# Strided heads before local heads, narrower first groups of expert 0, and q scaled by 0.125 on GpSimd when it is loaded

## The chip, the core and the metric

One core of a Trainium2 chip runs the whole program. The metric is the device time of one execution in microseconds (us). The engines are TensorE (PE, its weight loads PEld), VectorE (DVE), ScalarE (ACT), GpSimd (POOL) and SyncE (SP, which issues most transfers). Each engine works through its own list of instructions in the listed order.

## The reference

Attention over 2 images, 8 heads, 576 tokens of 64 dimensions: heads 0 to 3 see the last 32 tokens (local), heads 4 to 7 the earlier tokens of the same class modulo 32 (strided). Then a dense mixture of 8 experts whose weights P come from 8 rounds of row and column normalisation, and a second mixture that takes the two best experts of each token.

```python
scores = scale * np.matmul(q, k.transpose(0, 1, 3, 2))          # scale = 1/8
scores = np.where(masks[None, :, :, :], scores, -1000000000.0)
attn = np.exp(scores - np.max(scores, axis=-1, keepdims=True))
attn = attn / (np.sum(attn, axis=-1, keepdims=True) + 1e-09)
x = np.matmul(attn, v)                                           # heads side by side: 1152 x 512
P = np.exp(x @ w_gate - max)                                     # 8 rounds over rows, then columns
out = sum over e of P[:, e:e + 1] * (np.maximum(x @ w1[e], 0.0) @ w2[e])
```

The second mixture (`_moe2_ref`) is not touched.

## The kernel before

Products are made from a high and a low part of each operand (`split`: ACT writes the high part, DVE the low part), so that one wide product is three matmuls (`mm3`).

**Attention, one image at a time.** `attention(b)` runs two head pairs of local heads (`local_unit`, three groups of three blocks of 64 queries, six units in an image), then the strided heads (`strided_unit`, three units, each of both head pairs). Each unit does: mask and score matmuls into a PSUM bank (`scores`), row maxima on DVE (L241), the maxima times 0.125 on DVE (L242), exponentials with sums on ACT (L247, scale 0.125), then on DVE 1e-9 added to the sums (L248), reciprocals (L249) and the product (L251); transposes on PE into `tr`, a copy to `at` on ACT and DVE in turn, value matmuls into `ot`, and a split into `xh` and `xl`. The score banks come from the tags in `where[1]`: "ad" gives four banks, "a" two. It is set to "a" after image 0.

**Expert 0 is computed in an early and a late half.** While the attention of image 1 still runs, `pair1` and `pair2` make the hidden rows `gh`, `gl` (products `h`) and the outputs `y` for the tokens in `early`, then, after the gate and its rounds (`sinkhorn`, one matmul `cs` in each of the 8 rounds), those in `late`. Conversions of a weight block `raw` to `u1h`, `u1l`, `u2h`, `u2l` are placed behind the attention's splits (`firsts[8]` and later). `sums()` prepares `r`, `sh` and `sl` for experts 1 to 6, whose products are `a`, `b`, `c`, `d` (L715).

The order on each engine is fixed when the program is built: a scheduler goes by its own times of instructions, and `tc.issue_after` holds some back. The lines that the steps speak of:

```python
early = ((0, 512),)
late = ((512, 320), (832, 320))
    with tc.issue_after(marks[1]), tc.issue_after(lows[0].ins):
        sums()
```

Of the kernel before, what the change touches and what calls it, by code (L numbers as in the profile page):

```python
# [9 lines left out]
F32 = mybir.dt.float32  # L10
# [4 lines left out]
AF = mybir.ActivationFunctionType  # L15
# [5 lines left out]
STRIDE = 32  # L21
# [24 lines left out]
MASKED = -8.0e9  # L46
# [16 lines left out]
def tile_kernel(ctx: ExitStack, tc: tile.TileContext, qL, kL, vL, qS, kS, vS, wg, u12, w1, w2, wgn, noise, v1, v2, cst, masks, dummy, out):  # L63
# [117 lines left out]
    where = [0, "ad", None]  # L181
# [4 lines left out]
    def load_pair(b, hp):  # L186
        local = hp < 2
        nq, nk, nb, q, k, v = (NQ, LK, NJ, qL, kL, vL) if local else (GK, GK, NG, qS, kS, vS)
        hp %= 2
        flip[1] = (flip[1] + 1) % 4  # L190
        qs = acc[:, 4:].rearrange("p t d -> p (t d)")[:, flip[1] * 640:flip[1] * 640 + nb * nq]
        w = k.shape[-1]
        if b == 0 and not local:
            qs = pre.tile([128, NG * GK], F32, name=f"qs{hp}")
            ks = pre.tile([128, S + STRIDE], F32, name=f"ks{hp}")
        else:
            ks = apool.tile([128, S + STRIDE], F32, tag="ks", name="ks")
        if local or hp == 0:
            where[2] = (pre if b == 0 and not local else apool).tile([128, NG, 128], F32, tag="vs", name="vs")
        vs, n = where[2], v.shape[-2]  # L200
        if b == 0 and hp == 0 and local:
            cut = 3 * nq
            nc.sync.dma_start(ks[:, :224], k[b, hp, :, :224])
            nc.sync.dma_start(qs[:, :cut], q[b, hp, :, :cut])
            nc.sync.dma_start(ks[:, 224:w], k[b, hp, :, 224:])
            nc.sync.dma_start(qs[:, cut:], q[b, hp, :, cut:])
        else:
            nc.sync.dma_start(ks[:, :w], k[b, hp])
            nc.sync.dma_start(qs, q[b, hp])

        def values():
            if local:
                nc.sync.dma_start(vs[:, :n], v[b, hp])
            elif hp == 1:
                nc.sync.dma_start(vs[:, :n], v[b])

        return (qs, ks, vs), values
# [44 lines left out]
    def local_unit(b, hp, j0, nb, got):  # L262
        qs, ks, vs = got
# [18 lines left out]
    def strided_unit(b, j0, nb, pairs):  # L282
        mask = maskb[:, None, M_MS:].to_broadcast([128, nb, GK])
        scv = [scores(GK, GK, mask, j0, nb, qs, ks, GK) for qs, ks, _ in pairs]
        vs = pairs[0][2]
# [19 lines left out]
    def load_first():  # L305
        pairs, queue = [], []
        for hp in range(4):
            got, values = load_pair(0, hp)
            pairs.append(got)
            if queue:  # L310
                queue.pop(0)()
            queue.append(values)
        queue.pop()()
        return pairs

    def attention(b):
        pairs = load_first() if b == 0 else []

        def get(hp):
            while hp >= len(pairs):  # L320
                got, values = load_pair(b, len(pairs))
                values()
                pairs.append(got)
            return pairs[hp]
# [28 lines left out]
    where[1] = "a"  # L353
# [264 lines left out]
    early = ((0, 512),)  # L618
    late = ((512, 320), (832, 320))
# [27 lines left out]
    for q in range(NP):  # L647
        raw = fetch_u(0, q)
        with tc.issue_after(firsts[min(q, 1) * 3 + 8].ins):
            a, b = conv_u1(raw[0]), conv_u2(raw[1])  # L650
        pair1(a, early)
        for t in range(4):
            pair2(b, t, None, q == 0)
# [13 lines left out]
    def sums():  # L667
        with tc.tile_pool(name="tpool", bufs=1, side="right", reuse_waits="tile") as tpool:
            for c in range(2):
                r = tpool.tile([128, 4, HALF], F32, tag="r", name="r")  # L670
                for i in range(4):
                    nc.vector.tensor_tensor(r[:, i], quarter[0][i][:, c].bitcast(F32), quarter[1][i][:, c].bitcast(F32), op=ALU.add)
                for o, x, y, op in ((3, 2, 3, ALU.add), (2, 0, 2, ALU.subtract), (0, 3, 0, ALU.subtract), (1, 1, 0, ALU.subtract)):
                    nc.vector.tensor_tensor(r[:, o], r[:, x], r[:, y], op=op)
                for k, i in enumerate((3, 0, 2, 1)):
                    split(sh[:, k, c], sl[:, k, c], r[:, i])

    marks = []
    for q in range(NP):
        q = NP - 1 - q  # L680
        if q < NP - 1:
            raw = fetch_u(0, q)
            a, b = conv_u1(raw[0]), conv_u2(raw[1])
        pair1(a, late)
        for t in range(4, NT):
# [448 lines left out]
_HOST = ["qL", "kL", "vL", "qS", "kS", "vS", "wg", "u12", "w1", "w2", "wgn", "noise", "v1", "v2", "cst", "masks", "dummy"]  # L1134


def layout(x):
# [10 lines left out]
    def keys(a):  # L1148
        return a.transpose(0, 1, 3, 2).reshape(B, 2, 2 * D, a.shape[2])
# [25 lines left out]
    for j in range(3):  # L1175
# [15 lines left out]
    d = dict(qL=keys(q[:, :4]), kL=keys(kL), vL=values(vL, LK, NQ),  # L1191
             qS=keys(qS), kS=keys(kS), vS=values(vS, GK, GK).reshape(B, 128, NG, 2 * D), wg=rows(x["moe_w_gate"]),
# [22 lines left out]
```

## Time and profile before

| | before |
|---|---|
| median of 3 runs | 1104.33 us (1103.67 to 1104.6) |
| profiled execution, its time | 1105.53 us |
| span of the profiled execution | 1103.7 us |
| PE busy, share of the span | 1085.4 us, 98% |
| PEld | 954.5 us, 86% |
| DVE | 661.6 us, 60% |
| ACT | 396.5 us, 36% |
| POOL | 158.8 us, 14% |
| TensorE's granted clock, mean | 0.992 of full speed |

PE has work nearly all the time. A matmul's shown duration overlaps the next one, so that a busy PE is not a PE at its best: the spacing of starts tells more. Whatever is lost is lost in the first 180 us. The granted clock is there in fractions of 2.4 GHz, and 0.50 is 1.2 GHz.

### The profile page before, as it was taken

Reading aid. Unit: us, or ns where it says so; the run is one execution under the profiler, and the core shown is the slowest. Engines: PE = TensorE matmul, PEld = TensorE weight load, DVE = VectorE, ACT = ScalarE, POOL = GpSimd, SP = SyncE. Lnnn points to the kernel's source line nnn. Section 1 sums busy time; section 2 is a strip of 40 time slices with the busy share of each in tenths; the row PEclk is TensorE's granted clock in tenths of the full one; section 3 lists DMA queues with packets and bytes.
Section 4 is the critical chain, followed back from the end, with each engine's and each line's share of the span. In section 5 each row is a group of like instructions: output and inputs, shape, how many; then the busy total and the mean of one; then the engine's idle time right before and its main releaser. Section 6 shows DMA issues by size and latency. Waiting matters only on the chain.

```text
span 1103.7 us, 17178 instructions
## 1 busy us (share of the span) xinstructions
PE 1085.4 (98%) x6840; PEld 954.5 (86%) x6840; DVE 661.6 (60%) x1359; ACT 396.5 (36%) x893; POOL 158.8 (14%) x182
## 2 busy tenths in 40 slices
PE   9999999999999999999999999999999999999996
PEld 6778988999899999899999999988888888888885
DVE  6865896666666666666666666554266465445440
ACT  6641334332322333322332332222133254444541
POOL 1000112111111111121111120000041432232211
PEclk9999999999999999999999999999999999999998
DMA  9321162111111121111121111122103674666531
GB/s 349 133 77 39 39 198 67 39 71 44 40 39 39 39 78 39 39 39 39 39 77 39 39 39 39 39 77 77 39 21 125 181 256 106 205 204 205 185 99 24
DMA packets 31589, 98.18 MB, mean 89 GB/s; under 512 B 6482, under 2 KB 15186, under 8 KB 22928
## 3 DMA queue, kind: packets, MB, share of 16 engines
q1 hardware_dynamic: 16192, 78.94, 19.7%
q0 software_dynamic: 5408, 11.26, 4.9%
q10 hardware_dynamic: 9904, 6.83, 2.0%
q8 instruction: 55, 0.90, 0.3%
q14 instruction: 30, 0.25, 0.1%
HBM read 85.51 MB, written 11.60 MB: 88 GB/s over the span
## 4 chain that ended last, share of the span: by engine, by line
PE 90%; DVE 3%; DMA 2%; ACT 2%; issue 1%; POOL 1%; POOLq 0%; SPq 0%; ACTq 0%
PE y L164 42%; PE h L164 17%; PE a L715 14%; PE b L715 7%; PE d L715 3%; PE y L892 2%; PE xgt L800 1%; PE sc L232 1%; ACT spread L247 1%; DMA raw<-in_v 1%; DMA xg<-x2d,tt 1%; DVE wl L106 1%; PE sc L221 0%; POOL table L548 0%; PE lgT L367 0%
## 5 line engine op out<-in xcount | busy, mean ns | idle before, releaser
L641 DVE SCALAR_TENSOR_TENSOR acc<-y,P,acc 128x512 f32<-128x512 f32 x207 | 152.8, 748 | 142.8 <-PE y L164 142.7
L164 PE MATMUL y<-u2h,gh 128*128 128x512 f32 x504 | 199.0, 395 | 0.6 <-DVE acc L641 0.3
L164 PE MATMUL y<-u2l,gh 128*128 128x512 f32 x504 | 197.8, 392 | 0.0
L164 PE MATMUL y<-u2h,gl 128*128 128x512 f32 x504 | 190.6, 393 | 0.8 <-DVE gl L102 0.8
L154 POOL TENSOR_TENSOR ut<-raw 128x256 f32<-128x256 f32 x48 | 36.5, 782 | 554.0 <-DVE u1l L106 446.0
L164 PEld LDWEIGHTS y<-u2h,gl 128*128 128x128 f32 x504 | 94.8, 189 | 20.8 <-DVE gl L102 1.6
L164 PE MATMUL h<-xh,wh 128*128 128x384 f32 (+8 forms) x352 | 110.2, 313 | 0.2 <-DVE hl L102 0.2
L164 PE MATMUL h<-xl,wh 128*128 128x384 f32 (+8 forms) x352 | 110.2, 313 | 0.0
L164 PE MATMUL h<-xh,wl 128*128 128x384 f32 (+8 forms) x352 | 109.8, 312 | 0.0
L164 PEld LDWEIGHTS y<-u2h,gh 128*128 128x128 f32 x504 | 95.1, 189 | 16.2 <-issue 0.7
L164 PEld LDWEIGHTS y<-u2l,gh 128*128 128x128 f32 x504 | 95.0, 188 | 14.1
L101 ACT ACTIVATE hh<-h 128x256 fp32r<-128x256 f32 (+2 forms) x88 | 35.6, 415 | 95.5 <-PE h L164 95.5
L164 PEld LDWEIGHTS h<-xh,wh 128*128 128x128 f32 x352 | 66.4, 189 | 1.1 <-DVE hl L102 0.5
L164 PEld LDWEIGHTS h<-xl,wh 128*128 128x128 f32 x352 | 66.4, 189 | 0.9 <-issue 0.4
L104 ACT ACTIVATE u2h<-raw 128x1024 fp32r<-128x1024 f32 x31 | 33.0, 1064 | 94.5 <-PE y L164 90.8
L164 PEld LDWEIGHTS h<-xh,wl 128*128 128x128 f32 x352 | 66.4, 189 | 0.0
L102 DVE SCALAR_TENSOR_TENSOR hl<-h,hh 128x256 fp32r<-128x256 f32 (+2 forms) x88 | 40.3, 465 | 41.2 <-ACT hh L101 41.2
L106 DVE TENSOR_TENSOR wl<-raw,wh 128x1024 fp32r<-128x1024 f32 x42 | 49.5, 1221 | 22.8 <-ACT wh L104 22.8
L715 PE MATMUL b<-sh,u1h 128*128 128x288 f32 x192 | 57.5, 299 | 0.0
L715 PE MATMUL b<-sl,u1h 128*128 128x288 f32 x192 | 57.5, 299 | 0.0
L715 PE MATMUL b<-sh,u1l 128*128 128x288 f32 x192 | 57.4, 299 | 0.0
L715 PE MATMUL a<-sh,u1l 128*128 128x288 f32 x192 | 57.0, 297 | 0.0
(257 smaller groups left out, 2453.9 us busy)
## 6 DMA issues: line engine op xcount, KB each, us to landing
raw<-in_u SPq DMA_DIRECT2D x31, 1024.0 KB, 4.8
raw<-in_v SPq DMA_DIRECT2D x20, 1024.0 KB, 8.9
acc<-in_v SPq DMA_DIRECT2D x12, 1024.0 KB, 6.8
raw<-in_w SPq DMA_DIRECT2D x4, 1024.0 KB, 4.9
out<-zero ACTq DMA_DIRECT2D x1, 3072.0 KB, 18.2
vs<-in_vL SPq DMA_DIRECT2D x4, 576.0 KB, 7.1
x2d<-acc ACTq DMA_DIRECT2D x9, 256.0 KB, 2.0
vs<-in_vS SPq DMA_DIRECT2D x2, 704.0 KB, 6.5
```

What stands on the lines that cost most here:

```text
L101: seen[0] = nc.scalar.activation(hi, src, AF.Relu)
L102: lows.append(nc.vector.scalar_tensor_tensor(lo, src, 0.0, hi.bitcast(F32), op0=ALU.max, op1=ALU.subtract))
L104: seen[0] = nc.scalar.activation(hi, src, AF.Copy)
L106: nc.vector.tensor_tensor(lo, src, hi.bitcast(F32), op=ALU.subtract)
L154: nc.gpsimd.tensor_tensor(t[:, o], x, y, op=ALU.subtract)
L164: nc.tensor.matmul(o, a, b, start=start, stop=stop)
L232: nc.tensor.matmul(sc[h * 64:h * 64 + w, i * nk:(i + 1) * nk], qs[r, j * w:(j + 1) * w], ks[r, j * step:j * step + nk], start=False, stop= ...
L247: nc.scalar.activation(s[:, x, i], v[:, i], AF.Exp, scale=0.125, bias=nmx[:, k:k + 1], accum_out=sm[:, k:k + 1])
L641: nc.vector.scalar_tensor_tensor(acc[:, t], p, P[:, t, scale:scale + 1], acc[:, t], op0=ALU.mult, op1=ALU.add)
L715: nc.tensor.matmul(p, l[:, b, c], m, start=first and i == 0, stop=i == 5, skip_group_check=not first)
L800: nc.tensor.transpose(p[:, o:o + 128], xg[:, c * 128:(c + 1) * 128], ident)
L892: nc.tensor.matmul(p[j * w:j * w + k, :d], hr[:, f, :k], raws[f // 4][:, f % 4, j * d:(j + 1) * d], start=f == 0, stop=f == 7)
```

## The change

The strided heads of an image now come first, the local units after them, and of these both head pairs of one group of blocks in turn. Keys and queries come in one tensor per kind (`xS`, `xL`), strided ones of image 0 in two pieces; the queries are multiplied by 0.125 on GpSimd where they land (`scale`, nine instructions more on its list). L242 is gone, and the exponentials have no scale (the mask's constant is an eighth of what it was). The score banks go down to two ("a") already after the first local group of image 0. The early half of expert 0 is 384 tokens and three `y` tiles instead of 512 and four; the late half is two groups of 384 instead of two of 320, with six `y` tiles instead of five. The conversions of the first block are placed behind `firsts[4]` and `firsts[6]`, which are now the last strided unit and the first local one. `sums()` is tied to `marks[0]` and `marks[1]`, one half each.

```diff
-MASKED = -8.0e9
+MASKED = -1.0e9
...
-    def load_pair(b, hp):
...
+    def scale(x):
+        nc.gpsimd.tensor_scalar(x, x, 0.125, None, op0=ALU.mult)
+
+    def load_strided(b):
+        xs = [(pre if b == 0 else apool).tile([128, 2, NG * GK], F32, tag=f"x{hp}" if b == 0 else "x", name="x",
+                                              bufs=2 - (b == 0)) for hp in range(2)]
+        cut = STRIDED[0][1] * GK
+        for p in (slice(0, cut), slice(cut, NG * GK)) if b == 0 else (slice(0, NG * GK),):
+            for hp in range(2):
+                nc.sync.dma_start(xs[hp][:, :, p], xS[b, hp, :, :, p])
+                scale(xs[hp][:, 0, p])
...
+    def load_local(b):
+        xs, vs = [], []
+        for hp in range(2):
+            x = acc[:, 4:].rearrange("p t d -> p (t d)")[:, hp * 1280:hp * 1280 + 2 * S + STRIDE]
+            nc.sync.dma_start(x, xL[b, hp])
+            scale(x[:, :S])
...
-        nc.vector.tensor_scalar(nmx[:, :n], nmx[:, :n], 0.125, None, op0=ALU.mult)
...
-                nc.scalar.activation(s[:, x, i], v[:, i], AF.Exp, scale=0.125, bias=nmx[:, k:k + 1], accum_out=sm[:, k:k + 1])
+                nc.scalar.activation(s[:, x, i], v[:, i], AF.Exp, bias=nmx[:, k:k + 1], accum_out=sm[:, k:k + 1])
...
-        for hp in range(2):
-            for j0, nb in LOCAL:
-                local_unit(b, hp, j0, nb, get(hp))
-        get(3)
+        xs, vs, values = load_strided(b)
+        values()
+        lx, lv = load_local(b)
         for j0, nb in STRIDED:
-            strided_unit(b, j0, nb, pairs[2:])
+            strided_unit(b, j0, nb, xs, vs)
+        for j0, nb in LOCAL:
+            if j0:
+                where[1] = "a"
+            for hp in range(2):
+                local_unit(b, hp, j0, nb, *lx[hp], lv[hp])
...
-    where[1] = "a"
...
-    early = ((0, 512),)
-    late = ((512, 320), (832, 320))
+    early = whole[:1]
+    late = whole[1:]
...
-        with tc.issue_after(firsts[min(q, 1) * 3 + 8].ins):
-            a, b = conv_u1(raw[0]), conv_u2(raw[1])
+        with tc.issue_after(firsts[10 if q else 4].ins):
+            a = conv_u1(raw[0])
+        with tc.issue_after(firsts[10 if q else 6].ins):
+            b = conv_u2(raw[1])
...
+                with tc.issue_after(marks[c]):
+                    r = tpool.tile([128, 4, HALF], F32, tag="r", name="r")
...
-    with tc.issue_after(marks[1]), tc.issue_after(lows[0].ins):
-        sums()
+    sums()
```

On VectorE, among the local units of image 0, the list of before reads as follows (`nmx` are the maxima, `sm` the sums, `s` the weights of a unit; each unit has its own numbers):

```order
L248 TENSOR_SCALAR sm_186<-sm_186 128x3
L241 TENSOR_REDUCE nmx_255<-sc_244 128x3
L249 RECIPROCAL sm_186<-sm_186 128x3
L242 TENSOR_SCALAR nmx_255<-nmx_255 128x3
L251 TENSOR_TENSOR s_182<-s_182,sm_186 128x288
L248 TENSOR_SCALAR sm_222<-sm_222 128x3
L241 TENSOR_REDUCE nmx_289<-sc_280 128x3
```

The maxima of a unit two places on (255) stand between the sum and the product of unit 182. On the same engine, among the local units of image 0, the list now reads:

```order
L106 TENSOR_TENSOR xl_77<-ot_249,xh_76 128x12x18
L244 TENSOR_TENSOR s_397<-s_397,sm_400 128x288
L235 TENSOR_REDUCE nmx_431<-sc_422 128x3
L241 TENSOR_SCALAR sm_433<-sm_433 128x3
L242 RECIPROCAL sm_433<-sm_433 128x3
L106 TENSOR_TENSOR xl_77<-ot_305,xh_76 128x8x18
L244 TENSOR_TENSOR s_430<-s_430,sm_433 128x288
L106 TENSOR_TENSOR u1l_941<-raw_938,u1h_940 128x512 x2
L106 TENSOR_TENSOR xl_77<-ot_306,xh_76 128x8x18
L253 COPY at_411<-tr_407 96x384
L235 TENSOR_REDUCE nmx_464<-sc_455 128x3
```

The maxima of the next unit (431, 464) have moved behind the product of the unit before them, and a weight conversion stands between. On TensorE, at the first wide product of expert 0, before:

```order
L298 MATMUL ot_515<-at_512,vs_119 64x54 x6
L227 LDWEIGHTS mask_sb_103
L227 MATMUL sc_658<-mask_sb_103 128x288
L232 MATMUL sc_658<-ks_653,acc_75 64x96 x6
L227 LDWEIGHTS mask_sb_103
L227 MATMUL sc_692<-mask_sb_103 128x288
L232 MATMUL sc_692<-ks_653,acc_75 64x96 x6
L271 MATMUL tr_604<-cs_78,s_593 96x128 x3
L164 MATMUL h_972<-xh_76,u1h_962 128x512
```

and on TensorE at the same place now:

```order
L221 LDWEIGHTS mask_sb_103
L221 MATMUL sc_561<-mask_sb_103 128x216
L226 MATMUL sc_561<-x_535 54x54 x8
L269 MATMUL ot_479<-at_477,vs_122 64x64 x6
L263 MATMUL tr_506<-cs_78,s_496 96x128 x3
L164 MATMUL h_950<-xh_76,u1h_940 128x384
L164 MATMUL h_950<-xl_77,u1h_940 128x384
```

Before, all of image 0, five score groups of image 1 and two of its transposes stand ahead of the first `h`. Now two score groups of image 1 do, and one value group of image 0 (`ot_512`) comes after it.

## Rows read from the trace of the kernel before

**Rows 1.** Windows of 10 us: stretch, engines' busy us (instructions), clock, DMA share, GB/s.

```profile
10.00:20.00 10.00, 9.96 (x175) 7.26 (x173) 8.24 (x35) 8.65 (x49) 0.00 (x0) 1.00 1.03 411
...
140.00:150.00 10.00, 9.41 (x49) 7.73 (x49) 10.00 (x20) 5.06 (x9) 1.40 (x2) 1.00 0.34 115
...
160.00:170.00 10.00, 9.11 (x50) 7.14 (x49) 9.75 (x28) 3.21 (x7) 3.90 (x4) 1.00 1.03 319
170.00:180.00 10.00, 8.99 (x51) 8.73 (x52) 5.50 (x17) 2.66 (x7) 0.00 (x0) 0.83 0.12 49
```

**Rows 2.** Waits of TensorE in 0 to 200 us: total, times, longest.

```profile
PE cs L395 <- DVE c L393: 1.5, 1, 1.5
...
PE sc L227 <- ACT spread L247: 1.1, 2, 0.6
```

**Rows 3.** Windows of 0.5 us around slow clocks; the clock is third from the end.

```profile
34.50:35.00 0.50, 0.50 (x3) 0.40 (x2) 0.50 (x2) 0.50 (x2) 0.00 (x0) 0.63 0.00 0
...
65.50:66.00 0.50, 0.50 (x3) 0.37 (x3) 0.50 (x3) 0.00 (x0) 0.00 (x0) 0.59 0.00 0
...
68.50:69.00 0.50, 0.50 (x3) 0.40 (x2) 0.00 (x0) 0.50 (x4) 0.00 (x0) 0.50 0.00 0
...
174.50:175.00 0.50, 0.50 (x5) 0.50 (x4) 0.17 (x1) 0.30 (x1) 0.00 (x0) 0.68 0.00 0
```

**Rows 4.** Timeline of ScalarE: start, duration, line, operation, tiles, shapes, count.

```profile
8.18 0.34 ACT L247 ACTIVATE s<-sc,nmx 128x96 f32<-128x96 f32 x1 [6.16 <-DVE nmx L242]
8.51 0.33 ACT L247 ACTIVATE s<-sc,nmx 128x96 f32<-128x96 f32 x1
...
24.22 0.39 ACT L247 ACTIVATE spread<-sc,nmx 128x54 f32<-128x54 f32 x1
...
24.50 0.39 ACT L247 ACTIVATE spread<-sc,nmx 128x54 f32<-128x54 f32 x1
...
31.32 1.18 ACT L104 ACTIVATE u1h<-raw 128x512 fp32r<-128x512 f32 x2
32.35 1.08 ACT L104 ACTIVATE u2h<-raw 128x1024 fp32r<-128x1024 f32 x1
```

**Rows 5.** Timeline of VectorE in the attention of image 0.

```profile
25.97 0.17 DVE L248 TENSOR_SCALAR sm<-sm 128x3 f32<-128x3 f32 x1
26.17 0.18 DVE L249 RECIPROCAL sm<-sm 128x3 f32<-128x3 f32 x1
26.39 0.55 DVE L106 TENSOR_TENSOR xl<-ot,xh 128x216 fp32r<-128x216 f32 x1
26.86 0.43 DVE L251 TENSOR_TENSOR s<-s,sm 128x288 f32<-128x288 f32 x1
...
27.22 0.44 DVE L241 TENSOR_REDUCE nmx<-sc 128x3 f32<-128x288 f32 x1
...
28.59 0.55 DVE L260 COPY at<-tr 96x384 f32<-96x384 f32 x1
...
34.42 1.22 DVE L106 TENSOR_TENSOR u2l<-raw,u2h 128x1024 fp32r<-128x1024 f32 x1
```

**Rows 6.** Timeline of TensorE: a score group up to a transpose, and the first `h`.

```profile
10.27 0.28 PE L227 MATMUL sc<-mask_sb 128*128 128x288 bf16 x1
...
11.13 0.53 PE L271 MATMUL tr<-cs,s 128*96 128x128 f32 x3
...
33.83 0.78 PE L164 MATMUL h<-xh,u1h 128*128 128x512 f32 x1
```

**Rows 7.** GpSimd: a group of instructions (busy, mean ns, idle before), and a timeline row.

```profile
L347 POOL CAST upper<-cs 128x128 bf16<-128x128 f32 x1 | 0.3, 289 | 25.7 <-DMA cs<-in_cst 25.7
...
129.80 2.06 POOL L154 TENSOR_TENSOR ut<-raw,ut 128x256 f32<-128x256 f32 x2
```

**Rows 8.** Timeline of VectorE, one operation beside GpSimd's work and three without.

```profile
131.36 1.11 DVE L106 TENSOR_TENSOR sl<-r,sh 128x576 fp32r<-128x576 f32 x1
...
132.47 2.08 DVE L106 TENSOR_TENSOR sl<-r,sh 128x576 fp32r<-128x576 f32 x3
```

More of the change, by code (lines that the diff above doesn't have):

```diff
@@ L62, in tile_kernel @@
 @with_exitstack
-def tile_kernel(ctx: ExitStack, tc: tile.TileContext, qL, kL, vL, qS, kS, vS, wg, u12, w1, w2, wgn, noise, v1, v2, cst, masks, dummy, out):
+def tile_kernel(ctx: ExitStack, tc: tile.TileContext, xL, vL, xS, vS, wg, u12, w1, w2, wgn, noise, v1, v2, cst, masks, dummy, out):
     nc = tc.nc
@@ L180, in tile_kernel @@
     flip = [0, 0]
-    where = [0, "ad", None]
+    where = [0, "ad"]
     spread = [apool.tile([128, 4, 2, 64], F32, name=f"spread{i}", bufs=1) for i in range(2)]
@@ L184, in tile_kernel @@
         nc.gpsimd.memset(x, 0.0)
-    def load_pair(b, hp):
[L187 to L217, printed above, removed]
@@ new lines, in load_local @@
+    def load_local(b):
[4 more added lines that the diff above has]
+            scale(x[:, :S])
+            xs.append((x[:, :S], x[:, S:]))
+        for hp in range(2):
+            v = apool.tile([128, NG, 128], F32, tag="vs", name="vs", bufs=3)
+            nc.sync.dma_start(v[:, :NJ], vL[b, hp])
+            vs.append(v)
+        return xs, vs
@@ L260, in take, with local_unit @@
             nc.vector.tensor_copy(o, i)
[L262 to L263 removed]
+    def local_unit(b, hp, j0, nb, qs, ks, vs):
         first = maskb[:, M_ML:M_MS].rearrange("p (b k) -> p b k", b=3)
@@ L280, in local_unit, with strided_unit @@
         split(xh[:, hp, o], xl[:, hp, o], ot[:, :nb * NQ])
-    def strided_unit(b, j0, nb, pairs):
+    def strided_unit(b, j0, nb, xs, vs):
         mask = maskb[:, None, M_MS:].to_broadcast([128, nb, GK])
-        scv = [scores(GK, GK, mask, j0, nb, qs, ks, GK) for qs, ks, _ in pairs]
-        vs = pairs[0][2]
+        scv = [scores(GK, GK, mask, j0, nb, x[:, 0], x[:, 1], GK) for x in xs]
         wide = spread[where[0] // 2 % 2]
@@ L303, in strided_unit @@
             split(view[0][:, r0:r1], view[1][:, r0:r1], ot[:, :(r1 - r0) * NI].rearrange("p (r i) -> p r i", i=NI))
[L305 to L314, printed above, removed]
-    def attention(b):
[L317 to L324, printed above, removed]
-        for hp in range(2):
-            for j0, nb in LOCAL:
-                local_unit(b, hp, j0, nb, get(hp))
-        get(3)
-        for j0, nb in STRIDED:
-            strided_unit(b, j0, nb, pairs[2:])
+    def attention(b):
+        xs, vs, values = load_strided(b)
+        values()
+        lx, lv = load_local(b)
+        for j0, nb in STRIDED:
+            strided_unit(b, j0, nb, xs, vs)
+        for j0, nb in LOCAL:
+            if j0:
+                where[1] = "a"
+            for hp in range(2):
+                local_unit(b, hp, j0, nb, *lx[hp], lv[hp])
     mask_sb = apool.tile([128, NMASK // 2], F32, name="mask_sb", bufs=1)
@@ L648, in tile_kernel @@
         raw = fetch_u(0, q)
-        with tc.issue_after(firsts[min(q, 1) * 3 + 8].ins):
-            a, b = conv_u1(raw[0]), conv_u2(raw[1])
+        with tc.issue_after(firsts[10 if q else 4].ins):
+            a = conv_u1(raw[0])
+        with tc.issue_after(firsts[10 if q else 6].ins):
+            b = conv_u2(raw[1])
         pair1(a, early)
-        for t in range(4):
+        for t in range(3):
             pair2(b, t, None, q == 0)
@@ L669, in sums @@
             for c in range(2):
[L670 to L676, printed above, removed]
+                with tc.issue_after(marks[c]):
+                    r = tpool.tile([128, 4, HALF], F32, tag="r", name="r")
+                    for i in range(4):
+                        nc.vector.tensor_tensor(r[:, i], quarter[0][i][:, c].bitcast(F32), quarter[1][i][:, c].bitcast(F32), op=ALU.add)
+                    for o, x, y, op in ((3, 2, 3, ALU.add), (2, 0, 2, ALU.subtract), (0, 3, 0, ALU.subtract), (1, 1, 0, ALU.subtract)):
+                        nc.vector.tensor_tensor(r[:, o], r[:, x], r[:, y], op=op)
+                    for k, i in enumerate((3, 0, 2, 1)):
+                        split(sh[:, k, c], sl[:, k, c], r[:, i])
     marks = []
@@ L684, in tile_kernel @@
         pair1(a, late)
-        for t in range(4, NT):
+        for t in range(3, NT):
             pair2(b, t, None, q == NP - 1)
         marks.append(seen[0].ins)
-    with tc.issue_after(marks[1]), tc.issue_after(lows[0].ins):
-        sums()
+    sums()
     with tc.issue_after(seen[0].ins):
@@ L1190, in layout @@
     dummy[:, 0] = np.arange(E * ROWS) % ROWS % PAD
-    d = dict(qL=keys(q[:, :4]), kL=keys(kL), vL=values(vL, LK, NQ),
-             qS=keys(qS), kS=keys(kS), vS=values(vS, GK, GK).reshape(B, 128, NG, 2 * D), wg=rows(x["moe_w_gate"]),
+    d = dict(xL=np.concatenate([keys(q[:, :4]), keys(kL)], 3), vL=values(vL, LK, NQ),
+             xS=np.stack([keys(qS), keys(kS)], 3), vS=values(vS, GK, GK).reshape(B, 128, NG, 2 * D), wg=rows(x["moe_w_gate"]),
              u12=np.stack([x["moe_w1"].reshape(E, NC, 128, NP, 256).transpose(0, 3, 2, 1, 4).reshape(E, NP, 128, 2, 512),
```

4 lines of the change are left out of this document (3 added, 1 removed).

## The prediction

> **What bounds the kernel now.** The page comes first: TensorE is busy 98% of the span, so a gain has to come from time in which TensorE idles or runs at half its clock. The windows of 10 us show where that is [rows 1]. At 10 to 20 us TensorE counts as busy, but ScalarE is at 8.65 and VectorE at 8.24 of 10 us: there the chain score, maxima, exponentials, product, transpose sets the pace, and TensorE's 175 instructions are small ones. At 140 to 180 us TensorE idles .59, .89 and 1.01 us in three windows while VectorE is full (10.00 and 9.75). The 0.5-us windows add the clock [rows 3]: before 34.5, before 68.5 and before 174.5 us TensorE stood still or did little, and 0.50 to 0.68 of full speed was granted for about 3.3 to 3.7 us each time, which costs half of that, some 1.7 us. After 180 us I found no loss, and from about 215 us on the order of all engines is the same in both kernels. So the change is worth what it does to these first stretches. I went through them by a ledger: the time up to a point less the time that the columns done by then take at full clock. In the kernel before it stands at 9.2 us at 33.8, 12.9 at 70, 15.0 at 150 and 20.1 at 179.
>
> **The change part by part.** The columns of TensorE in sum hardly change: three groups of `h` are 3 x 384 columns instead of 512 + 2 x 320, and `y` has nine tiles in both. What changes is when there is work.
>
> **A, the front: +5.8 us.** I walked the new order by hand with durations of before. Removed: one operation on VectorE of .17 us, by the neighbouring 128x3 operation [rows 5], ahead of each unit's exponentials; the first exponential then starts at about 7.75 instead of 8.18 [rows 4]. The strided exponentials of 54 columns follow each other every .28 us, the local ones of 96 every .32 to .33 [rows 4]. The strided units of image 0 have 22: 7.75 + 22 x .28 = 13.9, and with one copy of .46 on ScalarE the first local unit starts at 14.4. So far nothing is lost. But now every local unit hangs on the one before it. In the kernel before, the maxima of a unit two places on stand between the sum and the product of a unit, so that ScalarE has its next exponentials ready. In the new order the maxima come behind the product of the preceding unit, and often behind its `xl`. One turn is then three exponentials, .95; the sum's tail, .1; the add .20; the reciprocal .22; `xl` .47; the product .36; the reduction .37 [rows 5]; and .1 to start: 2.75 us, in which ScalarE works about a third. From 14.4 two units in stock and then such turns give 18.7, 20.2 and 23.1. The next turn also has two pieces of `u1l` on VectorE, which I take at .6 each (half of the 1.22 us of `u2l`, which has twice the columns [rows 5]), a second `xl` and a copy: 27.9. The last has `u2l` of 1.2 behind `u2h` of 1.08 [rows 4, 5]: 32.1. With its exponentials, sum, `xl`, copy and product it ends at 34.75, its transposes take .46 to .53 [rows 6], and the first `h`, which stands behind these transposes, starts at 35.3 instead of 33.83: 1.5 us later. Less is done by then, too. Before, five score groups of image 1 of .86 each (11.13 - 10.27 [rows 6]) and two transposes of .46 stand ahead of it: 5.2. Now two strided score groups do, about 1.46, and a value group of .5 is still owed: .96. 1.5 + 5.2 - .96 = 5.8 us, rounded up. The bounds: each handoff up to .5 shorter for five turns, 3.2; or longer, where the nine scalings on GpSimd share time with VectorE, 7.3: GpSimd's subtraction runs up to 131.86 [rows 7], and beside it a two-input VectorE operation took 1.11 instead of .69 [rows 8], .41 on up to four operations.
>
> The scalings themselves (216 to 594 columns each) have no row. Between the 128x128 conversion at 289 ns and the 128x256 subtraction at 1.03 us [rows 7] they lie between .4 and 1.8 us. I take the lower half, since they have one input as the conversion has, and cost them at nothing: the local ones finish long before 14.4 and the first two lie behind the load of the mask. Were they at 1.8, the first exponential would start about 1 us later; that is in the bound 7.3. The Trainium skill (GPSIMD Engine Reference, Key points) says that GpSimd shares its SBUF interfaces with VectorE and that VectorE instructions with two SBUF inputs contend. By that rule, the trace agrees: 1.11 against .69 us. It speaks against moving a multiplication to GpSimd, and by it the sum goes up by 4 x .41 = 1.6, to 1109.3.
>
> **B, just behind the first `h`: +2.0 us.** The new order puts transposes and a score group of image 1 into the first groups of `h`. By the walk TensorE stands from 37.9 to 39.0 for the exponentials of the first strided unit of image 1, and from 39.6 to 40.45 for a copy `at` that stands behind `u1h` (1.1) and `u2h` (1.0) on ScalarE [rows 4]. The list of waits has none of the kernel before at this place; its two waits for `spread` [rows 2] belong to D. Bounds 0, where the scheduler's neighbours run in time, and 3.
>
> **C, the clock at the front: +1.7 us.** The walk is at full clock. The kernel before has one half-clock stretch that ends at 34.7 [rows 3]: its first `h` took .78 us [rows 6] where later ones take .4. The new front idles in every turn, so I take one such stretch, too, in which the `h` behind 35.3 run at half clock: 3.4 x .5. Bounds 0 and two stretches, 3.4. The Trainium skill (TensorE: Matmul & The Clock Gate, What's actually happening) has the throttled state as the default, which activity releases. By that rule, a front that idles more often runs longer at the low level, and this speaks against the change; with two stretches the sum is 1109.4.
>
> **D, image 1's end: -2.4 us.** At 62 to 69 the kernel before waits 1.1 us for strided exponentials [rows 2], since strided units stand last and nothing is left beside them, and the half clock follows [rows 3], 3.3 x .5 = 1.65: 2.75 in sum. In the new order strided units come first and local ones last, spread among `h`. I leave .3. Bounds -2.75 and 0.
>
> **E, the gate and the sums: -3.7 us.** At 140 to 180 the kernel before loses .59 + .89 + 1.01 = 2.49 us by idling [rows 1], 1.5 of it one wait for a round of the normalisation [rows 2], and 3.5 x .5 = 1.75 by the clock after it [rows 3]: 4.24. The reason is VectorE's load: `r` and `sl` (.69 to 1.11 each [rows 8]) lie in the same 40 us as the conversions and the rounds. In the new order the first half's `r` stands ahead of most of the late half. By counting the late half on both engines VectorE has about 58 us of work for 67 us of TensorE, where it was 55.5 for 55.6. I leave .5. Bounds -4.2 and -1, since the rounds are as serial as before and one of them may still come late.
>
> The sum: 5.8 + 2.0 + 1.7 - 2.4 - 3.7 = +3.4 us. The profiled execution took 1105.53, 1.2 above the median, and becomes 1108.9; on the median's basis 1104.33 + 3.4 = 1107.7.
>
> **The rivals.** A measurement of this kernel can tell about 0.2% from no change: faster means below 1102.1, slower above 1106.5.
>
> - The front stays fed. The scheduler put the maxima behind the product by its own times; if the real handoffs are shorter, ScalarE's own work decides. That is 7.75 + 19.9 (22 x .28, 36 x .32 and the copies) and the last tail, with the first `h` near 29.8. Then A is 29.8 - 33.8 + 4.3 = +.3 and B is 0; with C at 1.7 and D and E as above the sum is -4.1: 1100.2. For it: ScalarE is the busiest at 10 to 20 us even now [rows 1], and 2.2 us of small operations are gone. Against it: the add, reciprocal, product and reduction of a unit are 1.15 us in line [rows 5], and none of that has cover in the new list. Chance .30. It decides if a turn is under about 1.5 us.
> - Level. A turn is dearer than ScalarE's own work by half of what the walk says: A is 2.9 and B 1, which with C, D and E gives 2.9 + 1 + 1.7 - 2.4 - 3.7 = -.5: 1103.8. Chance .18.
> - The first weight block comes late. It has 7.3 MB of queries, keys and values ahead of it or with it on SyncE's queue. At 411 GB/s [rows 1] it lands at 21 to 22 and is needed at 24.4. At 265 GB/s it would land at 29.5, the first `h` would come 5 us later, and the time would be 1112.7. Chance .08; the same queue kept 411 in the kernel before.
> - That the change doesn't do what it says can be left out: the new order of both engines is as described.
>
> **How the numbers follow.** The forecast, 1107.7, has .44, with a range of its own from 1104.8 (A at 3.2) to 1111. The fed front has .30, level .18, the late block .08. The range is 1100.0 to 1111.0: it leaves out the late block and about the lower part of the fed front. Slower: .44 + .08 = .52; faster .30; within 0.2%: .18.
>
> **What would show it.** A: in the trace of the changed kernel ScalarE waits for `nmx` at each local unit of image 0 from about 15 us on, and the first `h` starts at 35.3; if it starts before 32, A is wrong. B: waits of `tr` and `ot` on ScalarE at 38 to 41. C: one stretch near half clock right after the first `h`. D: no wait for `spread` and full clock at 60 to 70. E: VectorE's busy time under 9 of 10 us at 140 to 170, the wait of 1.5 us for a round gone, and no half clock at 170 to 175. GpSimd: nine new rows of .4 to 1.8 us. What would make the prediction wrong is above all the size of a turn: half a microsecond in each of five turns is 2.5 us, more than the line between slower and level.

## The result and the profile after

The changed kernel took 1110.83 us (median of 6 runs, 1108.96 to 1112.89) against 1104.43 for the kernel before (median of 6, 1103.67 to 1105.72): a ratio of 1.006, 95% interval 1.0045 to 1.0074. It is 6.4 us slower. The forecast was 1107.7, 3.4 us slower, with a range up to 1111. Executions of one kernel lie up to 10 us apart here, by how long TensorE runs at half clock, so that kernels are compared by the ratio of their runs to runs of the kernel before on the same chip.

The profiled execution has a span of 1110.1 us, 6.4 more than before. The windows of 10 us (stretch, then busy us of TensorE, weight load, VectorE, ScalarE and GpSimd with instructions, granted clock, DMA share, GB/s), to be held against [rows 1]:

```profile
10.00:20.00 10.00, 9.69 (x129) 7.41 (x126) 5.96 (x19) 6.96 (x40) 5.45 (x4) 0.66 1.03 423
20.00:30.00 10.00, 8.27 (x106) 5.96 (x106) 7.43 (x22) 5.77 (x25) 1.51 (x1) 0.74 0.55 216
30.00:40.00 10.00, 10.00 (x103) 7.97 (x103) 5.55 (x17) 6.93 (x36) 3.31 (x2) 0.50 0.64 208
...
90.00:100.00 10.00, 9.41 (x34) 7.71 (x35) 8.42 (x16) 1.91 (x3) 0.00 (x0) 0.68 0.01 1
140.00:150.00 10.00, 10.00 (x53) 9.25 (x52) 8.86 (x21) 2.04 (x3) 0.32 (x1) 1.00 0.97 286
...
160.00:170.00 10.00, 10.00 (x53) 9.24 (x52) 6.41 (x18) 3.13 (x7) 0.00 (x0) 1.00 0.29 106
170.00:180.00 10.00, 10.00 (x65) 9.30 (x64) 8.39 (x16) 3.44 (x8) 2.88 (x4) 1.00 0.07 12
```

Three of these windows in the kernel before, which [rows 1] doesn't have:

```profile
20.00:30.00 10.00, 8.41 (x163) 6.29 (x160) 8.92 (x31) 8.61 (x47) 0.00 (x0) 1.00 0.90 337
30.00:40.00 10.00, 9.97 (x86) 7.57 (x82) 9.15 (x26) 8.61 (x33) 1.04 (x5) 0.83 0.30 108
90.00:100.00 10.00, 10.00 (x48) 7.92 (x47) 4.10 (x8) 1.20 (x3) 0.00 (x0) 1.00 0.30 105
```

The first three are worse than before. No engine is at its limit there: ScalarE is busy 5.8 to 7.0 of 10 us where it was 8.6, VectorE 5.6 to 7.4. TensorE looks full in two of them, but at half clock (0.50 to 0.74 in the mean) its instructions are shown longer: the first `h` takes .67 us in it, later ones .34. The window at 90 us is worse, too. The last three, where the kernel before idled, are clean: VectorE under 9 of 10 us, TensorE full, clock 1.00.

TensorE's waits of 0 to 200 us (total, times, longest), against [rows 2]:

```profile
PE y L164 <- DVE gl L102: 2.3, 1, 2.3
PE sc L221 <- ACT s L240: 1.6, 1, 1.6
PE sc L226 <- POOL x L187: 1.6, 2, 1.0
```

The wait of 1.5 us for a round of the normalisation and those for `spread` are gone. In their place are one of 2.3 us for a low part `gl`, one for the exponentials of a local unit and two for scaled queries.

Short windows at the edges of the half-clock stretches, against [rows 3]:

```profile
11.00:11.50 0.50, 0.50 (x11) 0.42 (x11) 0.44 (x2) 0.50 (x5) 0.00 (x0) 0.59 1.00 415
17.50:18.00 0.50, 0.50 (x16) 0.50 (x13) 0.14 (x1) 0.00 (x0) 0.00 (x0) 0.58 1.05 438
24.50:25.00 0.50, 0.50 (x8) 0.28 (x8) 0.50 (x2) 0.00 (x0) 0.00 (x0) 0.74 0.22 66
41.50:42.00 0.50, 0.50 (x3) 0.18 (x2) 0.50 (x2) 0.50 (x2) 0.50 (x2) 0.69 0.16 65
...
89.00:90.00 1.00, 0.00 (x0) 0.00 (x0) 1.00 (x3) 0.00 (x0) 0.00 (x0) 0.80 0.00 0
90.00:91.00 1.00, 0.41 (x1) 0.41 (x2) 1.00 (x3) 0.00 (x0) 0.00 (x0) 0.50 0.00 0
96.00:97.00 1.00, 1.00 (x5) 0.84 (x4) 0.32 (x1) 0.32 (x1) 0.00 (x0) 0.79 0.00 0
```

By all windows of 1 us there are three stretches: 6.8 us from 11 on, 17.1 from 24 on, 6.8 from 89 on. The kernel before had three of 3.4. The timelines of the front: the exponentials of three local units on ScalarE (the second and the last two of six), and the first `h` on TensorE ([rows 4, 6] before):

```profile
21.57 0.34 ACT L240 ACTIVATE s<-sc,nmx 128x96 f32<-128x96 f32 x1 [1.62 <-DVE nmx L235]
...
30.34 0.34 ACT L240 ACTIVATE s<-sc,nmx 128x96 f32<-128x96 f32 x1 [1.62 <-DVE nmx L235]
34.57 0.34 ACT L240 ACTIVATE s<-sc,nmx 128x96 f32<-128x96 f32 x1 [1.40 <-DVE nmx L235]
```

```profile
38.86 0.67 PE L164 MATMUL h<-xh,u1h 128*128 128x384 f32 x1
```

Each of these units waits 1.4 to 1.6 us for its maxima, as the walk had a wait in each turn. The first `h` starts at 38.86; before it was 33.83 and the forecast 35.3. At 90 us, VectorE and then TensorE:

```profile
87.98 2.08 DVE L649 TENSOR_TENSOR r<-xh,xl 128x576 f32<-128x576 f32 x3
89.99 0.55 DVE L102 SCALAR_TENSOR_TENSOR gl<-h,gh 128x384 fp32r<-128x384 f32 x1
```

```profile
90.59 0.79 PE L164 MATMUL y<-u2h,gl 128*128 128x512 f32 x1 [2.26 <-DVE gl L102]
```

Three pieces of `r`, 2.08 us, stand on VectorE ahead of the `gl` for which the next `y` waits. TensorE idles 2.26 us and runs at half clock behind it.

### The profile page after: what moved, and what is told of

The parts are those of the page before. It is cut to its first block, busy times and chain, and to the rows that moved or that the text cites. A ratio compares the mean times of both kernels' runs of the same rounds, so it can differ in the third digit from the quotient of the medians.

```text
span 1110.1 us, 17156 instructions
## 1 busy us (share of the span) xinstructions
PE 1091.8 (98%) x6840; PEld 964.4 (87%) x6840; DVE 662.9 (60%) x1341; ACT 396.7 (36%) x893; POOL 171.1 (15%) x192
## 4 chain that ended last, share of the span: by engine, by line
PE 92%; DMA 2%; DVE 2%; issue 1%; POOL 1%; ACT 1%; SPq 0%; POOLq 0%; ACTq 0%
PE y L164 43%; PE h L164 17%; PE a L691 14%; PE b L691 7%; PE d L691 3%; PE y L868 2%; PE sc L226 1%; PE xgt L776 1%; PE ot L269 1%; DMA acc<-in_xL 1%; DMA raw<-in_v 1%; DMA xg<-x2d,tt 1%; DVE wl L106 1%; PE tr L263 1%; POOL table L522 1%
## 5 line engine op out<-in xcount | busy, mean ns | idle before, releaser
L104 ACT ACTIVATE u1h<-raw 128x512 fp32r<-128x512 f32 (+1 forms) x62 | 30.6, 543 | 76.6 <-PE a L691 57.4
```

What stands on the lines that cost most here:

```text
L104: seen[0] = nc.scalar.activation(hi, src, AF.Copy)
```

## The experiments

**The wait for `gl`.** e5 is the changed kernel again, beside later runs on their chip. e2 adds one order edge to it; e6 and e11 add the same edge where the front has fillers, and are compared with e3 and e7, which have the fillers alone.

```
-                with tc.issue_after(marks[c]):
+                with tc.issue_after(marks[c]), tc.issue_after(lows[5 if c == 0 else 0].ins):
                     r = tpool.tile([128, 4, HALF], F32, tag="r", name="r")
```

> The changed kernel with the first half's r held behind the low part gl of the sixth hidden group (one more issue_after on VectorE). In the changed kernel three r operations (2.08 us) stand ahead of this gl, TensorE waits 2.3 us for it at 88.3 to 90.6, and runs at half clock from 89.8 to 96.8. Theory A, this wait and the clock behind it cost 2.3 + 3.4 = 5.7 us: both are gone and the time is 1105.1, the kernel before's within 1 us. Theory B, VectorE is full there anyway and the wait comes back one or two instructions later, at the logits' maximum or the next gl: TensorE waits 1 to 2 us at 90 to 105 and the time is 1108 to 1111.

> The changed kernel itself, as a control beside the next three: 1110 to 1113 us, with a wait of 2.3 us for gl at about 90 us and 24 us or so at half clock before 45 us. If it comes out under 1108 here, the gains read for the fillers and for gl were the chip's and not theirs.

> The fillers of the front (four matmuls of 512 columns ahead of each of the first twelve score groups) and r held behind the sixth gl, together, in the changed kernel. Theory A, two separate costs: with the fillers alone the profile had full clock all along and only the wait of 2.3 us for gl left, so that the time falls by a further 1.3 to 2.3 us, to 1.5 us or so below the kernel before's. Theory B, VectorE is full at 85 to 95 and the wait goes over to the logits' maximum, as the 1.0 us there with r held back alone: less than 1 us is gained and the time is that of the kernel before within 1 us.

e2 took 1.0040 of the kernel before (1.0027 to 1.0052), the control e5 1.0047 (1.0031 to 1.0063) with 1110.47 us. e6 against e3: 0.9989 (0.9977 to 1.0) and 1.0003 (0.9994 to 1.0012). e11 against e7 (below): 0.9964 and 0.9977. The differences are .07% to .14%, .8 to 1.5 us. In each pair the intervals overlap; that all three point the same way speaks for a small gain. They are far from the 5.7 us that idling and clock add up to in the profiled execution: theory B of e2 holds. The waits of e6 say why:

```profile
PE mxT L352 <- DVE mx L350: 1.0, 1, 1.0
...
PE y L164 <- DVE gl L102: 0.3, 1, 0.3
```

`r` is still due in those microseconds, and 1.3 of the 2.3 us come back at the logits' maximum and at `gl`. The half clock behind the wait is no fixed price either: 6.8 us in the changed kernel, 3.4 in e5 and e7, none in e3, with a wait of 2.3 us in each.

**Undoing parts of the front.** e1 takes the scaling back (no `scale`, L242 and the scale in the exponential as before); e4 keeps four score banks until image 1:

```
-            if j0:
-                where[1] = "a"
...
+    where[1] = "a"
     attention(1)
```

> The changed kernel with the scaling put back: no multiplication on GpSimd, the maxima times 0.125 on VectorE and the scale in the exponential as before; the order of the units and the groups of expert 0 stay changed. In the changed kernel TensorE stands from 7.6 to 9.8 us for scaled queries and the granted clock is 0.50 from 11.2 to 17.6 and from 24.7 to 41.5 us. Theory A, the scalings on GpSimd start the slow clock, and the slow clock makes the handoffs long: TensorE has no wait for GpSimd, the stretch at half clock from 11 us is gone, the first h starts at 36 us or sooner instead of 38.9, and the time is 1106 to 1108. Theory B, the handoffs between VectorE, ScalarE and TensorE are long by themselves and the slow clock follows them: at least 12 us at half clock stay, the first h starts at 38 or later, and the time is 1109 to 1112.

> The changed kernel with four score banks through all of image 0, as in the kernel before, instead of two after its first local group. By the order, the maxima of units two places on then stand ahead of the products again. Theory A, two banks make each local unit hang on the one before, 2.8 us a turn: the exponentials of the six local units follow with no wait over 1 us, the first h starts at 33 to 35 us instead of 38.9 and the time is 1105 to 1107. Theory B, the front is long by the scalings on GpSimd and the slow clock that follows them, whatever the banks: at least 10 us at half clock stay, the first h starts at 37 or later and the time is 1109 to 1112.

Neither was faster than the changed kernel: e1 1.0078 (1.0065 to 1.0091), e4 1.0087 (1.0072 to 1.0102). In e1 the first `h` starts at 33.45 and TensorE idles 2.2 us for a product at 45 to 47 instead (its profiled run took 1111.5 us, 3.4 under its median); in e4 half clock lasts for 27 us from 24 on. The theories are not told apart by this, since either edit lets the scheduler order everything anew: in e4 maxima do stand ahead of the product of the unit before, and the kernel loses elsewhere.

**Fillers on TensorE.** Matmuls that are overwritten keep TensorE working while it would wait:

```
-        hum(sc, 10 if where[0] == 1 else 2 if where[0] <= 4 else 0)
+        hum(sc, 10 if where[0] == 1 else 4 if where[0] <= 12 else 0)
```

The first score group keeps its ten in all kernels. e3 has four at each of the other eleven of image 0 (as shown: 38 matmuls more, not the 42 of the expectation), e7 at the other five strided ones (14 more), e8 at the six local ones (24 more), e12 at the second to sixth of the kernel before (14 more).

> The changed kernel with filling matmuls of 512 columns on TensorE: four ahead of each of the first twelve score groups (all of image 0) instead of two ahead of the second to fourth; 42 more, 9.7 us at full clock, their results are overwritten. Theory A, half of full clock in the front is what makes it long: the granted clock stays 1.00 from 5 to 45 us, the first h starts at 35 to 37 us instead of 38.9 although TensorE has more to do, and the time is 1107 to 1109. Theory B, the handoffs on VectorE and ScalarE set the front: the clock is full and the first h is still at 38 or later, and the time is 1110 to 1114.

> Fillers ahead of the six score groups of the strided units of image 0 alone (four each). If the slow clock at 24 to 42 us is the consequence of the one at 11 to 18, both are gone, the first h starts at 36 or sooner and the time is within 1 us of that with all fillers. If each stretch has its own cause (waiting for scaled queries at 7 to 10 us, and two-bank handoffs of the local units at 21 to 23 us), the first is gone, 15 us or more at half clock stay after 21 us, the first h starts at 37 to 38, and the time is 1 to 2 us below the changed kernel.

> Fillers ahead of the six score groups of the local units of image 0 alone (four each). If the stretch at 24 to 42 us is the dear one, it is gone although the one from 11 us may stay, the first h starts at 35.5 to 37, and the time is 2 to 4 us below the changed kernel. If the first stretch drags the second along, more than 10 us at half clock stay after 20 us and the gain is under 1 us.

> The kernel before with four filling matmuls ahead of each of its first six score groups (the local units of image 0) instead of two ahead of the second to fourth. If fillers help any front of this kind, the half clock at 31 to 35 us goes and the time is 1.5 to 2.5 us under the kernel before's. If they help only where the front idles before 24 us, as the changed one does, the time is that of the kernel before within 1 us, or longer by the 1 to 3 us that the fillers take.

e3: 1.0003 (0.9994 to 1.0012); e7: 0.9977 (0.9967 to 0.9988), faster than the kernel before; e8: 1.0000 (0.9989 to 1.0010); e12: 1.0030 (1.0018 to 1.0041), slower; its half clock at 31 to 35 is gone, and 6.8 us of it stand at 45 to 52. In e3, e7 and e8 there is no half clock before 80 us, and the first `h` starts at 35.09, 30.41 and 32.99. That looked like the clock's doing. But the first `h` of e7 is 5 us earlier than the walk at full clock had it, which no clock can give; and VectorE's list had changed beside the fillers.

**Order and fillers apart.** So the order was tied down: an edge from each instruction to the next, on VectorE, ScalarE and TensorE (fillers left free), in a sequence that another build had.

```
+    for eng, runs in PIN.items():
+        mine = [i for i in nc.cur_bb.bb.instructions if str(i.engine) == "EngineType." + eng
+                and type(i).__name__ != "BassTilePoolBoundary" and i.name not in hums]
+        line = [mine[k] for x, y in runs for k in range(x, y)]
+        for x, y in zip(line, line[1:]):
+            tc.add_manual_dep(y, x.name, mybir.DependencyInfo(mybir.DependencyClass.NoSync, mybir.DependencyReason.DATA),
+                              reason="pin")
```

e9 has the order of the changed kernel up to the first `h` and the fillers of e3; e10 the same order and no scaling at all:

> The changed kernel with the order of VectorE, ScalarE and TensorE up to the first hidden group tied to what it is there (extra order edges), and four filling matmuls ahead of each of the first twelve score groups on TensorE. The earlier fillers had also moved the scheduler's order; here only the fillers differ. Theory A, the slow clock is a cost of its own: no half clock before 45 us, the first h starts at 35 to 36 us as the walk at full clock had it, instead of 37.4 to 38.9, and the time is 2 to 4 us under the changed kernel's. Theory B, the gain of the fillers came from the order that the scheduler made of them: the clock is full and yet the first h starts at 37 or later, and the time is that of the changed kernel within 1 us.

> The changed kernel without the scaling on GpSimd, with the order of VectorE, ScalarE and TensorE up to the first hidden group tied to what it is with it. The scaling by 0.125 is left out and done nowhere else, so the weights are those of scores eight times as large; instructions and shapes are otherwise the same. Theory A, the scalings cost by what waits for them and by the slow clock that follows: TensorE's waits of 1.2 to 1.6 us at 7 to 10 us are gone, no half clock at 11 to 18, the first h starts at 35.5 to 37 and the time is 1 to 3 us under the changed kernel's. Theory B, the front hangs on the local handoffs and the scalings are hidden, as the prediction has it: half clock at 21 to 39 stays, the first h at 37 or later, and the time within 1 us of the changed kernel's.

e9: 1.0065 (1.0048 to 1.0082), its first `h` at 38.77 with one stretch of 3.4 us at half clock before it. The first local unit's exponentials came 1.5 us later than in the changed kernel (17.14 instead of 15.60), and behind the first `h`, where nothing was tied, it lost more (10 us at half clock from 45 on). So theory B holds for the first `h`, and the time says less than it should. e10: 1.0056 (1.0039 to 1.0074), first `h` at 39.09, half clock for 3.4 us from 13.5 and 17.1 us from 23.5 on. Without any scaling the changed order is as slow as with it: theory B of e10 holds. (Its first exponential began at 9.01 instead of 7.71, as the mask's matmuls came at 7.42 instead of 6.12: the ten opening fillers took 3.91 us in this execution and 2.63 in the changed kernel's. By the first local unit, 15.93 against 15.60, little of it was left.)

e13 and e14 complete the square, with the whole attention and early half tied: e13 the changed kernel's order with e7's fillers, e14 the order of e7 without its fillers.

> The changed kernel with its own order of VectorE, ScalarE and TensorE tied through the whole attention and early half, and the fillers of the run with strided fillers (four matmuls ahead of each of the first six score groups). If the order sets the front, the fillers gain nothing: the first h starts at 37 us or later and the time is the changed kernel's, 1110 to 1113. If the clock sets it, the first h starts at 35 to 36 and the time is 1106 to 1108.

> The changed kernel without additional fillers, but with the order of VectorE, ScalarE and TensorE that the scheduler made beside the strided fillers, tied through the attention and early half. If the order sets the front, the first h starts at 29 to 31 us as beside the fillers and the time is 1103 to 1106, 4 us or more under the changed kernel's. If the clock sets it, half clock is back at 11 to 18 and after 21 us, the first h starts at 33 or later and the time is 1108 to 1111.

| | no more fillers | 14 more fillers |
|---|---|---|
| order of the changed kernel | 1.0047 (e5) | 1.0049, 1.0036 to 1.0062 (e13) |
| order of e7 | 0.9998, 0.9982 to 1.0014 (e14) | 0.9977 (e7) |

The order is worth .5% without fillers and .7% with them, both clear of the intervals. The fillers give nothing in the one order and .2% in the other, where the intervals overlap. With the fillers is not the same as at full clock: e13 still has 10.2 us at half clock between 22 and 39 (e5 17). The first `h`, e13, then e14:

```profile
37.80 0.67 PE L165 MATMUL h<-xh,u1h 128*128 128x384 f32 x1
```

```profile
30.78 0.61 PE L165 MATMUL h<-xh,u1h 128*128 128x384 f32 x2
```

The exponentials of e14's local units on ScalarE:

```profile
19.87 0.34 ACT L242 ACTIVATE s<-sc,nmx 128x96 f32<-128x96 f32 x1 [0.25 <-DVE spread L246]
...
21.69 0.34 ACT L242 ACTIVATE s<-sc,nmx 128x96 f32<-128x96 f32 x1
...
24.40 0.34 ACT L242 ACTIVATE s<-sc,nmx 128x96 f32<-128x96 f32 x1
...
28.89 0.39 ACT L242 ACTIVATE s<-sc,nmx 128x96 f32<-128x96 f32 x1
```

One group waits .25 us, where each waited 1.4 to 1.6; the first `h` starts at 30.78, 7 us before e13's, although e14 ran at half clock from 11 to 18. Not all of the 7 us are time gained: in this order the first `h` stands ahead of the last local unit's transposes (36.48), in the changed one behind them (37.27 in e13). VectorE's list at this place in e14:

```
L244 RECIPROCAL sm_400<-sm_400 128x3
L107 TENSOR_TENSOR xl_77<-ot_249,xh_76 128x12x18
L237 TENSOR_REDUCE nmx_431<-sc_422 128x3
L246 TENSOR_TENSOR s_397<-s_397,sm_400 128x288
L107 TENSOR_TENSOR xl_77<-ot_305,xh_76 128x8x18
L237 TENSOR_REDUCE nmx_464<-sc_455 128x3
L243 TENSOR_SCALAR sm_433<-sm_433 128x3
```

The maxima 431 stand ahead of the product of the unit before, and 464 ahead of the sum, with the same two banks, the same conversions and the same scaling on GpSimd. e14 exchanges the lists of three engines together; the place of the maxima is the difference that the waits point at, and it wasn't moved alone.

**The fastest version.** e11 is e7 with `r` behind its `gl`; e15 the same order without e7's fillers.

> The changed kernel with four filling matmuls ahead of each of the six strided score groups of image 0, and r held behind the sixth gl. The fillers alone were 0.23% faster than the kernel before, with the wait of 2.3 us for gl and 3.4 us at half clock behind it left. Theory A: of these 2.3 + 1.7 = 4.0 us the logits' maximum takes 1.0 back, 3 us are gained, and the time is 0.4 to 0.6% under the kernel before's. Theory B: r later makes VectorE late for the rounds or the low parts after it, and the gain is under 1 us.

> As the run before it in this list (the order that the scheduler made beside the strided fillers, without them), and r held behind the sixth gl. With order the cause: 3 us under the same without r held back, 1101 to 1103, and 0.3 to 0.5% under the kernel before's. With the clock the cause: 1105 to 1108.

e11: 1103.26 us, 0.9964 (0.9951 to 0.9977) of the kernel before, the fastest here. e15: 0.9996 (0.9975 to 1.0017). Nine of its twelve runs took 1101.4 to 1103.0 us at a mean clock of 0.993 to 0.997, three 1112.2 to 1112.8 at 0.983 to 0.985. The profile is one of the three:

```profile
20.00:30.00 10.00, 10.00 (x110) 7.37 (x110) 6.36 (x20) 6.05 (x28) 1.17 (x1) 0.50 0.57 220
30.00:40.00 10.00, 10.00 (x117) 7.54 (x116) 6.63 (x19) 6.68 (x29) 4.21 (x7) 0.50 0.56 189
```

It has 31 us at half clock without a break and its first `h` at 36.52, where e11, with fillers and no half clock, has it at 29.19. All five runs of e11 lie between 1102.6 and 1104.4. The 3 us that were expected of `r` behind `gl` came in neither: e11 is 1.4 us under e7, and e15 beside e14 is .02% by the ratios, 1.6 us by the medians (1102.87 and 1104.49).

**Order and clock together.** The time from the second to the sixth local unit's exponentials, and TensorE's mean granted clock in it:

| run | order | from, to | us | clock |
|---|---|---|---|---|
| the changed kernel | its own | 21.57, 34.57 | 13.0 | 0.62 |
| e5 | its own | 19.29, 32.50 | 13.2 | 0.57 |
| e13 (fillers) | its own | 20.86, 33.99 | 13.1 | 0.81 |
| e9 (fillers) | its own | 22.57, 35.73 | 13.2 | 0.87 |
| e14 | that of e7 | 19.87, 28.89 | 9.0 | 1.00 |
| e15 (profile) | that of e7 | 18.98, 32.09 | 13.1 | 0.50 |

In the changed kernel's order these four turns take the same 13 us at any of these clocks; the walk had 13.4. There the chain over VectorE and ScalarE sets the pace. In the order of e7 they take 9.0 us at full clock and 13.1 at half. So the order of e7 shortens these turns at full clock only, and the clock matters where that chain doesn't set the pace. One profile stands behind each row. The ends of the row of e9, with its first `h`, and of e15:

```profile
22.57 0.34 ACT L242 ACTIVATE s<-sc,nmx 128x96 f32<-128x96 f32 x1 [1.60 <-DVE nmx L237]
...
35.73 0.34 ACT L242 ACTIVATE s<-sc,nmx 128x96 f32<-128x96 f32 x1 [1.40 <-DVE nmx L237]
```

```profile
38.77 0.42 PE L165 MATMUL h<-xh,u1h 128*128 128x384 f32 x1
```

```profile
18.98 0.34 ACT L242 ACTIVATE s<-sc,nmx 128x96 f32<-128x96 f32 x1
...
32.09 0.34 ACT L242 ACTIVATE s<-sc,nmx 128x96 f32<-128x96 f32 x1
```

## Why the prediction was half right

The same ledger as in the prediction, for both profiled executions, puts the 6.4 us in four places. It rests on one price per column, so that a step is good to about a microsecond only, and the changed kernel's profiled execution took 1111.87 us, 1.0 above the median.

- **A, the front: forecast +5.8, with C +7.5; measured +9.2.** The first `h` starts 5.0 us later (38.86 - 33.83) and has the 4.2 us less work behind it that the prediction counted. The mechanism was right, down to the turns: the walk had the exponentials of the last five local units at 18.7, 20.2, 23.1, 27.9 and 32.1. In e5, the same kernel without the first half-clock stretch, the four that wait are these:

```profile
19.29 0.34 ACT L240 ACTIVATE s<-sc,nmx 128x96 f32<-128x96 f32 x1 [1.61 <-DVE nmx L235]
23.45 0.34 ACT L240 ACTIVATE s<-sc,nmx 128x96 f32<-128x96 f32 x1 [1.39 <-DVE nmx L235]
28.08 0.34 ACT L240 ACTIVATE s<-sc,nmx 128x96 f32<-128x96 f32 x1 [1.63 <-DVE nmx L235]
32.50 0.34 ACT L240 ACTIVATE s<-sc,nmx 128x96 f32<-128x96 f32 x1 [1.60 <-DVE nmx L235]
```

With another order of the same instructions, e14, the turns take 9.0 us instead of 13 and the kernel is 5 us faster. That the order is the cause is shown; that it is the place of the maxima in it is read from lists and waits and wasn't tested by itself.

- **C, the clock: mis-sized.** The step let one stretch of 3.4 us fall on the `h` behind 35.3, 1.7 us. Measured were 24 us (17 in e5) at half clock before 42, most of it ahead of the first `h`. That doesn't cost half of 24: the four turns of the table above take 13 us at any of its clocks. The first `h` is 3.6 us behind the walk, 2.1 in e5. In the changed kernel 2.9 of them are there by the second unit (21.57 for the walk's 18.7), behind the stretch at 11 to 18; e5, at full clock there, is .6 late. And from the last exponentials to the first `h` the walk had 3.2 us: e9 takes 3.0 at full clock, the changed kernel 4.3 and e5 4.9 at half. The Trainium skill (TensorE: Matmul & The Clock Gate, What's actually happening) has the throttled state as the default that activity releases; the trace agrees, 24 us against 3.4 in the front of the kernel before, and the sum by this rule, 1109.4, was nearer than 1107.7.
- **B and D: forecast +2.0 and -2.4; measured -2.35 in all**, from the first `h` to the last value group of image 1. D's wait and half clock at 62 to 69 are gone as said. The waits of B didn't come: none at 38 to 41 in the list above. Of the copy's wait e5 has .4 us at 41.5, in front of a value group; why only that much came wasn't tested.
- **E, the gate and the sums: forecast -3.7; measured about -.5. This is the step that failed.** All that the kernel before lost from the rounds on, 6.1 us by the ledger (the step had 4.24), is gone, and VectorE's load is as forecast (8.86, 8.10 and 6.41 of 10 us at 140 to 170). But 5.6 us are new at 88 to 97: 2.26 of waiting and half of 6.8 at half clock (4.0 by the same count in e5, with 3.4 at half clock, so that E would be -2.1 there). The step compared sums of work over the late half, 58 us for 67, and said that `r` stands ahead of it. It didn't look at which instruction `r` stands ahead of: in VectorE's list three pieces of `r` are followed by the `gl` that TensorE needs next, and that row could be read before the run. Moving `r` behind it (e2, e6, e11) gives back .8 to 1.5 us, less than half of the 3.2 us that E fell short: the work of `r` is still due there, and for the rest the cause stays open. (In the prediction's reading of 140 to 180, VectorE is full in two of the three windows; in the third it is at 5.50.)

The sum of these is 9.2 - 2.35 - .5 = 6.35 us. Had E been 0 in the forecast, it would have been 7.1. That the forecast missed by 3 us and not by 5 is luck: B's 2.0 us, which didn't come, hid part of what C and E left out.

Of the rivals, the fed front was not this kernel, but it was possible: e14 and e7 are it. With the `gl` wait its time is the kernel before's and not 1100.2; without that wait and with fillers (e11) it is .36% or 4 us under it, about what that rival said. The first weight block was not late; no wait for it is in the lists. GpSimd's scalings were dearer than taken and yet no cost in this order. Timeline of GpSimd:

```profile
6.92 1.17 POOL L187 TENSOR_SCALAR x<-x 128x378 f32<-128x378 f32 x1
...
18.13 3.38 POOL L187 TENSOR_SCALAR x<-x 128x594 f32<-128x594 f32 x2 [2.79 <-DMA x<-in_xS]
31.20 1.66 POOL L187 TENSOR_SCALAR acc<-acc 128x576 f32<-128x576 f32 x1 [9.68 <-DMA acc<-in_xL]
```

There are ten, not nine (192 instructions on GpSimd for 182). They take .75 to 1.79 us, the whole of the range .4 to 1.8 and mostly its upper half; the local ones of image 0 run from 11.76 to 15.34, not long before 14.4. TensorE waits 1.6 us for them at 7 to 10 us. ScalarE has exponentials in stock then, and e10 without them is no faster. In e14 TensorE also waits 1.1 us, at 12 to 13, for a local scaling; what the scalings cost in that order wasn't tested.

## What to carry to other kernels

Where a scheduler sets the order, an edit changes two things, the work and the order, and undoing a part of it changes the order again: tie the order of the one build in the other before a difference is put down to the work. In a chain of small steps over three engines, look at which row stands directly ahead of the row that another engine waits for; sums of load over a stretch don't show it. The length of a wait and half of the slow stretch behind it are not its price: 5.7 us by that count were .8 to 1.5 when the wait was taken away, and the length of the slow stretch differs from run to run. A few fillers may be worth it for steadiness: in the order of e7, 4 of 24 runs without them took 1112 us or more, and none of 16 with them; that is too few to be sure.

## What had not been expected of the hardware

- One program (e15) took 1101.4 to 1103.0 us in nine runs and 1112.2 to 1112.8 in three, with a mean granted clock of 0.993 or more and 0.985 or less: some 10 us, with the clock as the only difference on record. Beside a wait of 2.3 us in an otherwise full stretch there were 6.8 us at half clock (the changed kernel), 3.4 (e5, e7) or none (e3).
- GpSimd's one-input scaling didn't slow VectorE's two-input operations, as its two-input subtraction had [rows 8]. The same product without it (e14, where GpSimd stands still from 15.01 to 18.02) and beside it (the changed kernel, where GpSimd scales from 11.76 to 15.34):

```profile
15.33 0.61 DVE L246 TENSOR_TENSOR spread<-spread,sm 128x432 f32<-128x432 f32 x1
```

```profile
13.03 0.61 DVE L244 TENSOR_TENSOR spread<-spread,sm 128x432 f32<-128x432 f32 x1
```

  The Trainium skill (GPSIMD Engine Reference, Key points) names contention with VectorE instructions that have two SBUF inputs. By that rule the sum would have risen by 1.6 us; here the measurement says no such thing for a one-input operation on GpSimd.
